# A longer opening in a new order, six column-halved weight blocks and paddings on two engines, in an attention-plus-bilinear-feed-forward kernel

## The chip, the cores and the metric

One core of a Trainium2 chip; the rounds of runs were on different chips, so a run is best compared with the kernel before in the same rounds (the ratio), and medians of different rounds only roughly. The metric is the device time of one execution in microseconds (us), of which a median is given. The granted clock is the share of full speed at which TensorE was let run; its mean over an execution is given where it matters. Engines: PE is TensorE (PEld its weight loads), DVE is VectorE, ACT is ScalarE, POOL is GpSimd, which issues the loads here, and SP is SyncE, which issues the DMA transposes. "Pair" means two attention heads of one batch: 4 pairs for each batch, 32 in all.

## The reference, cut to what matters

```python
# q, k, v: (batch 8, heads 8, seq 576, dim 64); bias_table: (32 buckets, 8 heads)
scores = matmul(q, k^T) / 8 + bias[head, bucket(|i - j|)]
attn   = softmax(scores);  attn_out = matmul(attn, v)
x   = attn_out as (4608 tokens, 512)
out = ((x @ w_a) * (x @ w_b)) @ w_out       # w_a, w_b: 512x1536, w_out: 1536x512
```

The softmax is computed as exp(score) times exp(bias); the exponentiated biases are read as sliding windows (tiles `W`) of a small table that the kernel itself writes to DRAM (`bias_tab`).

## The kernel before

Work runs in two parts. The opening (batch 0 and most of batch 1) is a list of tokens, issued in that order into each engine's queue. After it a loop over pairs takes over, which mixes attention steps with fixed numbers of feed-forward "units". Each engine's compute instructions run in the order of its queue; one that waits holds those behind it.

```python
    XG = [wpool.tile([128, 5, 2, Dh], BF16, name=f"XG{i}") for i in range(2)]   # attention output
    ...
    opening = """
        <k0 <q0 <q123h0 <tk <k23 <k1 <W0 <v0 <vtb <Wtb <W1 <W3 <vta <W2 <tq <R1 <q123h1 <v1 <R0 <Wta
        <wa0 <wb0 TK0 PD0 CK0:A PD1 w1 TQ0 PU1 CQ00:D CQ01:D w4 S000 w2 PU0 TQ20 E000 ...
        ... MT5 HA5b S62 E63 FA6b G5b MT6
        AV50 HA6b M63 E62 S60 FB6b N50 E60 FA7b G6b AV51 M62 HA7b FB7b M60 FA8f G7b N51 FB8f HA8f G8f
    """
    # <x: a load.  <W0..3: upper parts of the bias windows of pairs 0..3, <R0..3: the lower parts
    # S scores (PE), E exponentials (ACT), M bias products (DVE), T/ET/MT the same for the 64 tail
    # rows, AV attention times v (PE), N normalisation into XG (DVE), X transposes of XG (PE),
    # FA/FB products with w_a, w_b (PE), HA copy (ACT), G product (DVE), FO/HO w_out,
    # TH transposes of batch 2's q and k (DMA), w<n>: n filler matmuls on zeros
    # :A / :D: on ScalarE / VectorE.  FA3a, FA3b: column halves of weight block 3; FA8f: whole
    ...
    def av_norm(p, jqs):                     # token N: pav -> XG[p % 2]
        xg = XG[p % 2]
        ...
    def t_x(p, jqs=range(5), eng=None):      # XG -> xn, the feed-forward's input
        if 4 <= p < NP - 1 and p != 7:       # two DMA transposes, issued by SP
            nc.sync.dma_start_transpose(out=xn_sb[hp][...], in_=XG[p % 2][:, 0:4, :, :]...)
            nc.sync.dma_start_transpose(out=xn_sb[hp][...], in_=XG[p % 2][0:ST, 4, :, :]...)
            return
        tr_x(p, jqs); copy_x(p, jqs, eng)    # on PE, then a copy
    ...
    for s in range(7, NP + 1):               # loop step s: scores of pair s, av and N of pair s-1
        ...
```

Pair p writes its output to `XG[p % 2]`, and may do so only when pair p - 2's transposes have read it. And all DMA transposes stand in one queue, SP's, with batch 2's three transposes (`TH`: KB, QB, ZB) ahead of pair 5's.

The softmax here doesn't subtract the row's maximum and nothing guards it: scores larger than these inputs give would overflow.

Of the kernel before, what the change touches and what calls it, by code (L numbers as in the profile page):

```python
# [13 lines left out]
def kernel(  # L14
# [80 lines left out]
    vm = [wpool.tile([128, H, NM, Dh + 1], BF16, name=f"vm{i}") for i in range(2)]  # L95
    vt = [wpool.tile([128, H // 2, 2, Dh + 1], BF16, name=f"vt{i}") for i in range(2)]

# [70 lines left out]
    def load_vt(b):  # L168
        for hh in range(2):
            nc.gpsimd.dma_start(  # L170
                out=vt[b % 2][64 * hh:64 * hh + 64, :, hh, 0:Dh],
                in_=v[b, hh:H:2, SM:S, :].transpose([1, 0, 2]))
# [31 lines left out]

# [34 lines left out]

    nc.sync.dma_start(out=tab.ap(), in_=tab_sb[0:H, :])  # L240
    pad_vt(0)
    pad_ones(0)

# [5 lines left out]
    def load_vt_part(b, hh):  # L249
        nc.gpsimd.dma_start(  # L250
            out=vt[b % 2][64 * hh:64 * hh + 64, :, hh, 0:Dh],
            in_=v[b, hh:H:2, SM:S, :].transpose([1, 0, 2]))
# [85 lines left out]
    def copy_k(p, eng):  # L338
        copy(eng, KT[p % 4][:, :, :], st[p]["tk"][:, 0:SM].rearrange("d (t c) -> d t c", t=NM))

    def t_q(p, eng=None):
        if p >= NP or not early(p // 4):
            return
        ps = tr_half()
        transposes(ps, qn, p)
        copy(eng, QT[p % 4][:, :, :].rearrange("d a c -> d (a c)").rearrange("d (p t) -> d p t", t=NM),
             ps[:, 0:SM].rearrange("d (t p) -> d p t", t=NM))

    def t_k(p, eng=None, pool=None):
        if p >= NP or not early(p // 4):  # L350
            return
        ps = pool.tile([128, 1024], BF16, tag="ffn", name=f"trk{p}") if pool else tr_half()
        transposes(ps, kn, p)
        copy(eng, KT[p % 4][:, :, :], ps[:, 0:SM].rearrange("d (t c) -> d t c", t=NM))

# [198 lines left out]
    def av_mm(p, jqs, pool=None, tag="av"):  # L554
        b, hp = divmod(p, 4)
        i = b % 2
        pav = (pool or ps_av).tile([128, 3, 2, Dh + 1], FP32, tag=tag, name=f"av{p}_{jqs[0]}")
        for slot, jq in enumerate(jqs):
            nc.tensor.matmul(out=pav[:, slot, :, :], lhsT=weights_tail(p, jq),  # L559
                             rhs=vt[i][:, hp, :, :], start=True, stop=True)  # L560
            if jq == 4:
                for t in range(NM):
                    nc.tensor.matmul(out=pav[:, slot, :, :], lhsT=weights_last(p, t),  # L563
                                     rhs=vm[i][:, 2 * hp:2 * hp + 2, t, :], start=False,
                                     stop=True, skip_group_check=True)
# [25 lines left out]
    def t_x(p, jqs=range(5), eng=None):  # L591
        b, hp = divmod(p, 4)
        c0 = SM * B + ST * b
        if 4 <= p < NP - 1 and p != 7:
            nc.sync.dma_start_transpose(
# [95 lines left out]
    for c in range(NCH):  # L691
        if c == 0:
            parts = [(range(0, 8), 0, 256), (range(0, 8), 256, 256), (range(8, NDF), 0, 512)]
        else:
            parts = [(range(NDF), 0, 512)]
# [22 lines left out]
    def v_next(s):  # L718
# [9 lines left out]
    opening = """  # L728
        <k0 <q0 <q123h0 <tk <k23 <k1 <W0 <v0 <vtb <Wtb <W1 <W3 <vta <W2 <tq <R1 <q123h1 <v1 <R0 <Wta
        <wa0 <wb0 TK0 PD0 CK0:A PD1 w1 TQ0 PU1 CQ00:D CQ01:D w4 S000 w2 PU0 TQ20 E000 PC1 TQ10 S001 CQ20:D  # L730
        CQ10:D TQ30 E001 PC0 TZ1 CQ30:D S011 CZ1:A PC2 <vt1b <uq <vt1a <R2 <wa1 <q4 <R3 <k4 <wb1 <vb1b
        <q5 <k5 <uk <vb1a <wb2 <q6 <q7 <k6 <k7 <wa2 <wo S010 PF0 TK3 PF1 E011 TK2 CK3:D CK2:D E010 w1
        S300 M001 TK1 E300 M000 KS CK1:D EK w1 S101 V0:D E101 w1 S100 E100 M101 w1 S200 AV00 M300 E200 S301
        N00 TZ0 E301 M100 X00 S201 CX00:D AV10 wa4 E201 M200 N10 CZ0:A M201 X10 TQ11 M301 CX10:A T0 CQ11:A
        V1:D TQ31 ET0 S111 M010 AV20 E111 PW MT0 T1 N20 AV30 CQ31:A ET1 M011 TQ21 LH S110 N30 X20 CQ21:A
        S310 CX20:A MT1 X30 E110 AV01 CX30:D M111 FA0a E310 M110 S210 FB0a N01 HA0a S211 E210 FA1a G0a
        AV11 HA1a M210 E211 X01 T2 N11 TZ0x CX01:A T3 ET2 FB1a M211 X11 FA2a G1a CX11:A S311 MT2 HA2a
        FB2a ET3 CZ0x:D AV21 G2a E311 M310 TQ4 FA3a N21 CQ4:A TK4 FB3a HA3a CK4:D X21 FA4a G3a CX21:A
        S41 M311 HA4a S43 E41 MT3 FB4a FA5a E43 G4a AV31 LV M41 HA5a S40 V3:D S42 N31 E40 FB5a TQ5 G5a
        E42 X31 FA6a CQ5:D FB6a HA6a CX31:D TK5 G6a TZ1x CK5:A FA7a M40 FB7a HA7a CZ1x:D S52 S53 G7a E52  # L740
        FA0b V2:D FB0b M42 HA0b T4 E53 G0b FA1b M52 FB1b HA1b S50 M53 ET4 FA2b G1b TQ6 M43 HA2b S51
        CQ6:A FB2b MT4 E51 TQ7 G2b AV40 CQ7:D E50 TK6 M51 TK7 CK6:A FA3b M50 FB3b HA3b CK7:D S61 G3b T5
        E61 N40 FA4b FB4b HA4b M61 T6 ET5 G4b AV41 FA5b ET6 N41 TH S63 FB5b MT5 HA5b S62 E63 FA6b G5b MT6
        AV50 HA6b M63 E62 S60 FB6b N50 E60 FA7b G6b AV51 M62 HA7b FB7b M60 FA8f G7b N51 FB8f HA8f G8f
    """
# [4 lines left out]
    def step(token):  # L750
# [67 lines left out]
        elif kind == "N":  # L818
            av_norm(p, jqs)
            if not first and i[1] == 1:  # L820
                t_x(p)
        elif kind == "X":
            tr_x(p, jqs)
        elif kind == "CX":
            copy_x(p, jqs, eng)
        elif kind == "PU":
            pad_z(1, p)
        elif kind == "PF":
            nc.vector.memset(tl[0][64 * p:64 * p + 64, :, :, Dh - Dh * p:128 - Dh * p], 0.0)
        elif kind == "PC":  # L830
            if p == 2:
                pad_ones(1)
            else:
                nc.vector.memset(vt[1][64 * p:64 * p + 64, :, 1 - p, :], 0.0)
        elif kind == "PW":
            nc.vector.tensor_copy(out=Wt_sb[:, :, 0:64], in_=Wt_sb[:, :, 64:128])
        elif kind == "PD":
            pad_x(p)
        elif kind == "LH":
            load_half(2, 0)  # L840
            load_half(2, 1)
        elif kind == "TH":
            t_half(2, 0)
        elif kind == "LV":
            load_vt(2)
        else:
            raise ValueError(token)
# [4 lines left out]

    quotas = {7: 9, 8: 9}
    load_slot = {bb: 9 if bb == 3 else 12 if bb == 4 else 4 * bb - 5 for bb in range(3, B)}
    for s in range(7, NP + 1):
        new = s < NP
        U = "unit"
        A = lambda *jq: (lambda: av(s - 1, jq))
        steps = []
        if new:  # L860
            steps += [lambda: (qk(s, 0), ex(s, 0))]
        if new:
            head = [U, lambda: ex(s, 1), A(0, 1, 2), U, lambda: mul(s, 0), lambda: t_q(s + 1), U,
                    lambda: mul(s, 1)]
            late = [A(3, 4), lambda: t_x(s - 1), U]
            if s == 8:
                late = [A(3, 4), U, lambda: t_x(7, (0, 1, 2)), U, lambda: t_x(7, (3, 4))]
            if shared(s):
                pair = [lambda: v_next(s), lambda: (qk(s, 2), ex(s, 2), ex_rows(s)), U,
                        lambda: ex(s, 3), U, lambda: mul(s, 2), lambda: mul_rows(s)]  # L870
            else:
                pair = [lambda: v_next(s), lambda: (qk(s, 2), ex(s, 2)), U, lambda: ex(s, 3),
                        lambda: t_k(s + 1, ACT), U, lambda: mul(s, 2)]
            tail = [lambda: (qk_tail(s), ex_tail(s)), U, U, lambda: mul_tail(s)]
# [61 lines left out]
```

## Time and profile before

| | before |
|---|---|
| time, median of 3 | 416.77 us (416.66 to 417.65) |
| profiled span (an execution of 416.01 us, not one of the three) | 414.2 us |
| TensorE busy | 403.8 us, 97% |
| fillers on zeros | 22 matmuls |
| changes of the array's shape (rows x columns in use) from one matmul to the next | 177 |

The busy table and the chain of the page of the kernel before: engines with busy time, share and number of instructions; then the shares of the chain of work that ended last.

```profile
PE 403.8 (97%) x3497; PEld 210.9 (51%) x3497; DVE 241.1 (58%) x568; ACT 251.3 (61%) x388; POOL 133.5 (32%) x191
PE 90%; DMA 3%; POOL 2%; ACT 2%; issue 1%; ACTq 0%; DVE 0%
```

TensorE bounds the kernel. "97% busy" does not mean that only 3% can be won: the busy time of a matmul includes the run-out of its pipeline. The useful measure is from one matmul's start to the next one's. Here is one line of the timeline of the kernel before (start, duration, engine, line, operation, count):

```profile
71.86 1.89 PE L670 MATMUL po<-wo,g 128*128 128x512 bf16 x8
```

Eight matmuls of 512 columns take 1.89 us, of which the last one's own duration is 0.38 us: (1.89 - 0.38) / 7 = 0.216 us from start to start. The rest of the 0.38 us, 0.16 us, is run-out, which overlaps the next matmul.

The same kernel by stretches: us from the start, then length, and for each engine busy time and number of instructions, the granted clock, the DMA share and GB/s.

```profile
0.00:30.00 30.00, 24.56 (x330) 14.25 (x331) 21.73 (x65) 21.67 (x32) 22.51 (x36) 1.00 1.14 163
30.00:70.00 40.00, 39.22 (x472) 26.36 (x469) 33.45 (x87) 32.30 (x54) 24.90 (x35) 1.00 1.48 177
70.00:75.00 5.00, 5.00 (x30) 2.17 (x28) 2.59 (x8) 1.98 (x4) 0.78 (x2) 1.00 1.82 178
75.00:80.00 5.00, 5.00 (x61) 3.18 (x59) 3.13 (x9) 2.35 (x3) 1.22 (x2) 1.00 1.11 199
```

TensorE has gaps before 30 us and almost none after. So what a new order of this kind can win lies in the opening, a few us at most.

### The profile page before, as it was taken

To read this page: it belongs to the slowest core of one execution; us is meant where nothing else is said; L and a number is where in the kernel's file an instruction comes from. 1 tells how busy PE (TensorE), PEld (TensorE's weight loads), DVE (VectorE), ACT (ScalarE), POOL (GpSimd) and SP (SyncE) were. 2 spreads that over 40 slices of the span, in tenths; PEclk is the share of its full clock that TensorE was granted. 3 is DMA by queue.
4 is the path that set the end of the run, shared out by engine and by line. 5 is a ranking of instruction groups with operands and counts; after the bars stand their busy time and mean duration, and the time that the engine had idled before them with its cause. 6 is when DMAs were issued, how large, how long until landed. Compare 5 with 4: busy or idle time off the path is not lost.

```text
span 414.2 us, 8826 instructions
## 1 busy us (share of the span) xinstructions
PE 403.8 (97%) x3497; PEld 210.9 (51%) x3497; DVE 241.1 (58%) x568; ACT 251.3 (61%) x388; POOL 133.5 (32%) x191
## 2 busy tenths in 40 slices
PE   8789999999999999999999999999999999999996
PEld 3467664545454455544555555554545555444443
DVE  5778887466764665477646774567646652421320
ACT  4988876486647676676667665866476742322321
POOL 7956546399209500870059003400000000000000
PEclk9999999999999999999999999999999999999999
DMA  9999999999949943996099707940421012002004
GB/s 116 171 210 191 205 157 144 164 142 138 123 96 163 121 82 71 150 128 112 15 162 157 112 16 140 124 92 17 101 82 16 17 40 78 0 2 102 1 2 101
DMA packets 135786, 42.05 MB, mean 102 GB/s; under 512 B 113688, under 2 KB 130968, under 8 KB 135744
## 3 DMA queue, kind: packets, MB, share of 16 engines
q0 software_dynamic: 81712, 20.27, 54.6%
q1 hardware_dynamic: 48592, 11.87, 18.1%
q10 hardware_dynamic: 5440, 9.34, 6.8%
q8 instruction: 27, 0.44, 0.5%
q14 instruction: 15, 0.12, 0.1%
HBM read 39.18 MB, written 9.45 MB: 117 GB/s over the span
## 4 chain that ended last, share of the span: by engine, by line
PE 90%; DMA 3%; POOL 2%; ACT 2%; issue 1%; ACTq 0%; DVE 0%
PE pb L633 23%; PE pa L633 23%; PE po L670 22%; PE av L569 7%; PE qk L406 7%; DMA wb<-in_moe_w_b_dram 3%; PE av L559 2%; PE av L563 2%; PE qkt L479 1%; POOL W L235 1%; DMA bias_tab<-wo 1%; PE trb L306 1%; PE trb L415 1%; PE warm L220 1%; ACT att L514 1%
## 5 line engine op out<-in xcount | busy, mean ns | idle before, releaser
L430 ACT ACTIVATE at<-qk 128x1024 bf16<-128x1024 f32 x112 | 113.5, 1030 | 26.4 <-PE qk L406 10.6
L643 DVE TENSOR_TENSOR g<-pb,ha 128x512 bf16<-128x512 f32 (+1 forms) x116 | 75.9, 654 | 74.7 <-PE pb L633 46.8
L633 PE MATMUL pb<-xn,wb 128*128 128x512 bf16 (+1 forms) x464 | 112.5, 365 | 0.8 <-DMA wb<-in_moe_w_b_dram 0.8
L633 PE MATMUL pa<-xn,wa 128*128 128x512 bf16 (+1 forms) x464 | 112.5, 365 | 0.0
L640 ACT ACTIVATE ha<-pa 128x512 f32<-128x512 f32 (+1 forms) x116 | 66.7, 575 | 65.0 <-PE pa L633 65.0
L670 PE MATMUL po<-wo,g 128*128 128x512 bf16 x420 | 99.0, 379 | 0.0
L435 DVE TENSOR_TENSOR at<-at,W 128x1024 bf16<-128x1024 bf16 x112 | 74.8, 684 | 18.2 <-ACT at L430 18.2
L633 PEld LDWEIGHTS <-wa 128*128 128x128 bf16 x464 | 42.0, 98 | 46.2 <-issue 6.0
L633 PEld LDWEIGHTS <-wb 128*128 128x128 bf16 x464 | 41.4, 97 | 43.0 <-issue 4.7
L670 PEld LDWEIGHTS <-g 128*128 128x128 bf16 x420 | 38.7, 98 | 44.0 <-issue 2.5
L675 ACT ACTIVATE ob<-po 128x512 f32<-128x512 f32 x35 | 21.1, 601 | 40.7 <-PE po L670 34.4
L569 PE MATMUL av<-vm,at 128*128 128x65 bf16 x896 | 41.2, 194 | 0.0
L170 POOL DMA_DIRECT2D vt<-in_v_dram x12 | 7.4, 621 | 104.1 <-PE av L563 103.2
L580 DVE RECIPROCAL rc<-av 128x6 f32<-128x6 f32 (+1 forms) x64 | 11.9, 186 | 49.5 <-PE av L569 43.8
L569 PEld LDWEIGHTS <-at 128*128 128x128 bf16 x896 | 37.2, 98 | 6.2
L132 POOL DMA_DIRECT2D qn<-in_q_dram x48 | 36.8, 832 | 9.9 <-PE pb L633 6.8
L141 POOL DMA_DIRECT2D kn<-in_k_dram x48 | 36.4, 820 | 2.0 <-PE pb L633 1.4
L559 PE MATMUL av<-vt,att 128*128 128x130 bf16 x152 | 33.3, 219 | 0.0
L406 PE MATMUL qk<-QB,KB 64*128 64x512 bf16 x192 | 29.2, 381 | 0.2 <-ACT att L506 0.2
L582 DVE TENSOR_TENSOR XG<-av,rc 128x384 bf16<-128x384 f32 (+1 forms) x64 | 27.1, 424 | 2.2
L506 ACT ACTIVATE att<-qkt 128x640 bf16<-128x640 f32 x24 | 16.9, 702 | 12.9 <-PE qkt L480 12.9
L559 PEld LDWEIGHTS <-att 128*128 128x128 bf16 x152 | 15.0, 98 | 6.4
(104 smaller groups left out, 325.2 us busy)
## 6 DMA issues: line engine op xcount, KB each, us to landing
out_dram<-ob ACTq DMA_DIRECT2D x32, 256.0 KB, 2.6
vn<-in_v_dram POOLq DMA_DIRECT2D x16, 256.0 KB, 5.6
kn<-in_k_dram POOLq DMA_DIRECT2D x48, 64.0 KB, 4.6
qn<-in_q_dram POOLq DMA_DIRECT2D x48, 64.0 KB, 4.3
wa<-in_moe_w_a_dram POOLq DMA_DIRECT2D x3, 512.0 KB, 9.3
wb<-in_moe_w_b_dram POOLq DMA_DIRECT2D x3, 512.0 KB, 10.4
wo<-in_moe_w_out_dram POOLq DMA_DIRECT2D x1, 1536.0 KB, 15.5
xn<-XG SPq DMA_TRANSPOSE x52, 4.1
```

The source lines that it names most:

```text
L132: nc.gpsimd.dma_start(out=by_tile(qn[b % 2])[:, h0 // 4, t, :, :], in_=q[b, h0:h1, 128 * t:128 * t + 128, :].transpose([1, 0, 2]))
L141: nc.gpsimd.dma_start(out=by_tile(kn[b % 2])[:, h0 // 4, t, :, :], in_=k[b, h0:h1, t:SM:NM, :].transpose([1, 0, 2]))
L406: nc.tensor.matmul(out=ps[:, hh, :], lhsT=kT[r, t, :], rhs=qT[r, :, :], start=True, stop=True)
L430: nc.scalar.activation(out=at[:, :, :], in_=ps[:, :, :], func=ACTF.Exp, scale=scale)
L435: nc.vector.tensor_tensor(out=at[:, :, :], in0=at[:, :, :], in1=w[:, :, S - 1 + t:S - 1 + t - SM:-1], op=MULT)
L559: nc.tensor.matmul(out=pav[:, slot, :, :], lhsT=weights_tail(p, jq), rhs=vt[i][:, hp, :, :], start=True, stop=True)
L569: nc.tensor.matmul(out=pav[:, slot, hh, :], lhsT=weights(p, t, hh, jq), rhs=vm[i][:, 2 * hp + hh, t, :], start=False, stop=True, skip_grou ...
L582: nc.vector.tensor_tensor(out=xg[:, jqs[0]:jqs[0] + m, :, :], in0=pav[:, 0:m, :, 0:Dh], in1=rc[:, 0:m, :].unsqueeze(3).to_broadcast([128, ...
L633: nc.tensor.matmul(out=ps[:, 0:n], lhsT=w[df // 4][:, mc, 128 * (df % 4):128 * (df % 4) + 128], rhs=xn_sb[mc][:, 512 * c + lo:512 * c + lo ...
L640: nc.scalar.activation(out=ha[:, 0:n], in_=ff["pa", df, lo][:, 0:n], func=ACTF.Copy)
L643: nc.vector.tensor_tensor(out=g_sb[df][:, lo:lo + n], in0=ff["pb", df, lo][:, 0:n], in1=ff["ha", df, lo][:, 0:n], op=MULT)
L670: nc.tensor.matmul(out=po[:, :], lhsT=g_sb[df][:, 128 * tt:128 * tt + 128], rhs=wo_sb[:, df, :], start=(df == 0), stop=(df == NDF - 1))
```

## The change

Its intent: order the whole opening, now to the end of batch 1, by a list scheduler, so that TensorE has work at all times with fewer fillers; column halves only for six weight blocks; paddings with zeros on whichever of ScalarE and VectorE is free.

```diff
@@ paddings: a copy of zeros on ScalarE, or a memset on VectorE, as the token says
+    def pad(eng, x, p0, p1):
+        if eng is nc.vector:
+            nc.vector.memset(x, 0.0)
+            return
+        ... z = zero_sb (as fp32 where x is fp32), shaped like x
+        nc.scalar.activation(out=x, in_=z, func=ACTF.Copy)
@@ the ones of both buffers are set first
+    pad_ones(0)
+    pad_ones(1)
@@ pair 7 now has its own tokens (X70, X71: on PE, as before)
-        if 4 <= p < NP - 1 and p != 7:
+        if 4 <= p < NP - 1:
@@ six blocks in halves
-            parts = [(range(0, 8), 0, 256), (range(0, 8), 256, 256), (range(8, NDF), 0, 512)]
+            parts = [(range(0, 6), 0, 256), (range(0, 6), 256, 256), (range(6, NDF), 0, 512)]
@@ the opening, a new list (cut)
-        <k0 <q0 <q123h0 <tk <k23 <k1 <W0 <v0 <vtb <Wtb <W1 <W3 <vta <W2 <tq <R1 <q123h1 <v1 <R0 <Wta
-        <wa0 <wb0 TK0 PD0 ...
+        <k0 <q0 <q123h0 <k1 <k23 <vtb <W0 <tk <W2 <W1 <v0 <vta <W3 <tq <v1 <Wtb <q123h1 <R0 <Wta <k4 <R1
+        <wa0 <wb0 <R2 <uq <q4 ... PU0:A PV1:A PC1:A PF0:D TK0 PV0:A CK0:A PX1:D PF1:D w2 ...
+        HA0a T3 MT2 E210 AV11 CK4:D CX01:A S211 N11 FB0a ET3 FA1a G0a E211 X11 ...
+        V3:D HA5b M70 ET5 S71 N40 FB5b FA6f E71 MT5 G5b TQ6 HA6f M71 AV41 CQ6:A S73 N41 TH S72 E73 FB6f
+        E72 T6 M73 AV50 G6f ET6 M72 S62 FA7f N50 E62 MT6 AV51 HA7f M62 S61 S60 N51 E61 FB7f E60 S63 M61
+        FA8f G7f E63 M60 T7 HA8f FB8f M63 ET7 AV60 G8f FA9f MT7 N60 FB9f HA9f AV70 G9f FA10f N70 FB10f
+        HA10f AV71 G10f FA11f N71 FB11f HA11f X71 AV61 G11f X70 FO00 N61 FO01 CX71:D CX70:D FO02 HO0
@@ the loop starts one pair later; from step 9 on nothing differs
-    for s in range(7, NP + 1):
+    for s in range(8, NP + 1):
@@ (also: the layout of the value tails vt, and helpers that are no longer used)
```

More of the change, by code (lines that the diff above doesn't have):

```diff
@@ L95 @@
     vm = [wpool.tile([128, H, NM, Dh + 1], BF16, name=f"vm{i}") for i in range(2)]
-    vt = [wpool.tile([128, H // 2, 2, Dh + 1], BF16, name=f"vt{i}") for i in range(2)]
+    vt = [wpool.tile([128, 2, H // 2, Dh + 1], BF16, name=f"vt{i}") for i in range(2)]
     QT = [wpool.tile([128, NM, 128], BF16, name=f"QT{i}") for i in range(4)]
@@ L170, in load_vt @@
             nc.gpsimd.dma_start(
-                out=vt[b % 2][64 * hh:64 * hh + 64, :, hh, 0:Dh],
+                out=vt[b % 2][64 * hh:64 * hh + 64, hh, :, 0:Dh],
                 in_=v[b, hh:H:2, SM:S, :].transpose([1, 0, 2]))
@@ L191, in pad_tl, with pad_vt, pad_blocks, pad_x @@
         nc.vector.memset(tl[i][64:128, :, :, 0:Dh], 0.0)
-    def pad_vt(i):
-        nc.vector.memset(vt[i][0:64, :, 1, :], 0.0)
-        nc.vector.memset(vt[i][64:128, :, 0, :], 0.0)
+    def pad(eng, x, p0, p1):
+        if eng is nc.vector:
+            nc.vector.memset(x, 0.0)
+            return
+        n = int(np.prod(x.shape[1:]))
+        z = (zero_sb.bitcast(FP32) if x.dtype == FP32 else zero_sb)[p0:p1, 0:n]
+        if len(x.shape) == 3:
+            z = z.rearrange("p (a b) -> p a b", b=x.shape[2])
+        elif len(x.shape) == 4:
+            z = z.rearrange("p (a b c) -> p a b c", b=x.shape[2], c=x.shape[3])
+        nc.scalar.activation(out=x, in_=z, func=ACTF.Copy)
+    def pad_vt(i, hh, eng):
+        pad(eng, vt[i][64 * hh:64 * hh + 64, 1 - hh, :, :], 64 * hh, 64 * hh + 64)
+    def pad_blocks(x, hh, eng):
+        o = (Dh - Dh * hh) // 2
+        pad(eng, x.bitcast(FP32)[64 * hh:64 * hh + 64, :, :, o:o + Dh // 2], 64 * hh, 64 * hh + 64)
     def pad_ones(i):
-        nc.vector.memset(vt[i][0:64, :, 0, Dh:Dh + 1], 1.0)
-        nc.vector.memset(vt[i][64:128, :, 1, Dh:Dh + 1], 1.0)
+        nc.vector.memset(vt[i][0:64, 0, :, Dh:Dh + 1], 1.0)
+        nc.vector.memset(vt[i][64:128, 1, :, Dh:Dh + 1], 1.0)
         nc.vector.memset(vm[i][:, :, :, Dh:Dh + 1], 1.0)
-    def pad_x(i):
-        nc.vector.memset(XG[i][64:128, 4, :, :], 0.0)
+    def pad_x(i, eng):
+        pad(eng, XG[i][64:128, 4, :, :], 64, 128)
     nc.sync.dma_start(out=bt_sb[0:NB, :], in_=bias_table)
@@ L240 @@
     nc.sync.dma_start(out=tab.ap(), in_=tab_sb[0:H, :])
-    pad_vt(0)
-    pad_ones(0)
     def load_wt(hh):
@@ L250, in load_vt_part @@
         nc.gpsimd.dma_start(
-            out=vt[b % 2][64 * hh:64 * hh + 64, :, hh, 0:Dh],
+            out=vt[b % 2][64 * hh:64 * hh + 64, hh, :, 0:Dh],
             in_=v[b, hh:H:2, SM:S, :].transpose([1, 0, 2]))
@@ L339, in copy_k @@
         copy(eng, KT[p % 4][:, :, :], st[p]["tk"][:, 0:SM].rearrange("d (t c) -> d t c", t=NM))
-    def t_q(p, eng=None):
-        if p >= NP or not early(p // 4):
-            return
-        ps = tr_half()
-        transposes(ps, qn, p)
-        copy(eng, QT[p % 4][:, :, :].rearrange("d a c -> d (a c)").rearrange("d (p t) -> d p t", t=NM),
-             ps[:, 0:SM].rearrange("d (t p) -> d p t", t=NM))
-    def t_k(p, eng=None, pool=None):
-        if p >= NP or not early(p // 4):
-            return
-        ps = pool.tile([128, 1024], BF16, tag="ffn", name=f"trk{p}") if pool else tr_half()
-        transposes(ps, kn, p)
-        copy(eng, KT[p % 4][:, :, :], ps[:, 0:SM].rearrange("d (t c) -> d t c", t=NM))
     tz = {}
@@ L559, in av_mm @@
             nc.tensor.matmul(out=pav[:, slot, :, :], lhsT=weights_tail(p, jq),
-                             rhs=vt[i][:, hp, :, :], start=True, stop=True)
+                             rhs=vt[i][:, :, hp, :], start=True, stop=True)
             if jq == 4:
@@ L728 @@
     opening = """
-        <k0 <q0 <q123h0 <tk <k23 <k1 <W0 <v0 <vtb <Wtb <W1 <W3 <vta <W2 <tq <R1 <q123h1 <v1 <R0 <Wta
-        <wa0 <wb0 TK0 PD0 CK0:A PD1 w1 TQ0 PU1 CQ00:D CQ01:D w4 S000 w2 PU0 TQ20 E000 PC1 TQ10 S001 CQ20:D
-        CQ10:D TQ30 E001 PC0 TZ1 CQ30:D S011 CZ1:A PC2 <vt1b <uq <vt1a <R2 <wa1 <q4 <R3 <k4 <wb1 <vb1b
-        <q5 <k5 <uk <vb1a <wb2 <q6 <q7 <k6 <k7 <wa2 <wo S010 PF0 TK3 PF1 E011 TK2 CK3:D CK2:D E010 w1
-        S300 M001 TK1 E300 M000 KS CK1:D EK w1 S101 V0:D E101 w1 S100 E100 M101 w1 S200 AV00 M300 E200 S301
@@ L734 @@
-        N00 TZ0 E301 M100 X00 S201 CX00:D AV10 wa4 E201 M200 N10 CZ0:A M201 X10 TQ11 M301 CX10:A T0 CQ11:A
-        V1:D TQ31 ET0 S111 M010 AV20 E111 PW MT0 T1 N20 AV30 CQ31:A ET1 M011 TQ21 LH S110 N30 X20 CQ21:A
-        S310 CX20:A MT1 X30 E110 AV01 CX30:D M111 FA0a E310 M110 S210 FB0a N01 HA0a S211 E210 FA1a G0a
-        AV11 HA1a M210 E211 X01 T2 N11 TZ0x CX01:A T3 ET2 FB1a M211 X11 FA2a G1a CX11:A S311 MT2 HA2a
-        FB2a ET3 CZ0x:D AV21 G2a E311 M310 TQ4 FA3a N21 CQ4:A TK4 FB3a HA3a CK4:D X21 FA4a G3a CX21:A
@@ L739 @@
-        S41 M311 HA4a S43 E41 MT3 FB4a FA5a E43 G4a AV31 LV M41 HA5a S40 V3:D S42 N31 E40 FB5a TQ5 G5a
-        E42 X31 FA6a CQ5:D FB6a HA6a CX31:D TK5 G6a TZ1x CK5:A FA7a M40 FB7a HA7a CZ1x:D S52 S53 G7a E52
-        FA0b V2:D FB0b M42 HA0b T4 E53 G0b FA1b M52 FB1b HA1b S50 M53 ET4 FA2b G1b TQ6 M43 HA2b S51
-        CQ6:A FB2b MT4 E51 TQ7 G2b AV40 CQ7:D E50 TK6 M51 TK7 CK6:A FA3b M50 FB3b HA3b CK7:D S61 G3b T5
-        E61 N40 FA4b FB4b HA4b M61 T6 ET5 G4b AV41 FA5b ET6 N41 TH S63 FB5b MT5 HA5b S62 E63 FA6b G5b MT6
@@ L744 @@
-        AV50 HA6b M63 E62 S60 FB6b N50 E60 FA7b G6b AV51 M62 HA7b FB7b M60 FA8f G7b N51 FB8f HA8f G8f
+        <k0 <q0 <q123h0 <k1 <k23 <vtb <W0 <tk <W2 <W1 <v0 <vta <W3 <tq <v1 <Wtb <q123h1 <R0 <Wta <k4 <R1
+        <wa0 <wb0 <R2 <uq <q4 <q7 <k5 <q5 <R3 <wa1 <wb1 <k6 <vb1a <uk <vt1b <k7 <vt1a <wa2 <wb2 <vb1b
+        <q6 <wo PU0:A PV1:A PC1:A PF0:D TK0 PV0:A CK0:A PX1:D PF1:D w2 TQ0 PX0:A PU1:D CQ00:D PC0:D w2
+        S001 CQ01:A S000 E001 TQ20 TQ10 TK1 CQ10:A CQ20:D S011 E000 CK1:D TQ30 CQ30:A S100 E011 TK3 TK2
@@ new lines @@
+        CK3:D E100 S101 M001 TZ1 CK2:D E101 S301 M000 CZ1:D E301 w1 S201 M100 E201 w2 KS M101 EK w1 S200
+        M201 V0:D E200 S010 AV00 M301 E010 AV10 M200 TZ0 N00 S300 CZ0:A N10 E300 X00 V1:D X10 T0 CX00:D
+        AV20 CX10:A M300 ET0 TQ21 N20 TQ11 AV30 M010 CQ11:A CQ21:A S110 M011 PW:A S111 TQ31 LH E110 N30
+        X20 MT0 CX20:A T1 CQ31:D E111 AV01 M110 ET1 X30 M111 TK4 T2 N01 CX30:A S210 ET2 FA0a MT1 X01
+        HA0a T3 MT2 E210 AV11 CK4:D CX01:A S211 N11 FB0a ET3 FA1a G0a E211 X11 TZ0x M210 FB1a S310
@@ new lines @@
+        CZ0x:D HA1a S311 CX11:A G1a FA2a M211 E310 TQ4 TK5 MT3 AV21 HA2a CK5:D CQ4:A M310 FB2a E311 TQ5
+        G2a S43 CQ5:A N21 S42 FA3a E42 TQ7 M311 X21 FB3a HA3a CX21:D AV31 LV E43 G3a M42 FA4a CQ7:A M43
+        S41 HA4a S40 N31 E41 FB4a FA5a G4a E40 TK6 M41 X31 FB5a HA5a CX31:D S52 S53 G5a E52 FA0b M40
+        FB0b V2:D HA0b S51 G0b E53 FA1b CK6:D FB1b M52 HA1b TK7 E51 TZ1x G1b FA2b CZ1x:D FB2b HA2b S50
+        CK7:D FA3b G2b E50 M53 T4 FB3b M51 HA3b S70 ET4 G3b FA4b M50 FB4b HA4b T5 MT4 E70 FA5b G4b AV40
@@ L819, in step @@
             av_norm(p, jqs)
-            if not first and i[1] == 1:
+            if 4 <= p < 7 and i[1] == 1:
                 t_x(p)
@@ L825, in step @@
             copy_x(p, jqs, eng)
+        elif kind == "PV":
+            pad_vt(0, p, eng)
+        elif kind == "PC":
+            pad_vt(1, p, eng)
         elif kind == "PU":
-            pad_z(1, p)
+            pad_blocks(ZB[1], p, eng)
         elif kind == "PF":
-            nc.vector.memset(tl[0][64 * p:64 * p + 64, :, :, Dh - Dh * p:128 - Dh * p], 0.0)
-        elif kind == "PC":
-            if p == 2:
-                pad_ones(1)
-            else:
-                nc.vector.memset(vt[1][64 * p:64 * p + 64, :, 1 - p, :], 0.0)
+            pad_blocks(tl[0], p, eng)
+        elif kind == "PX":
+            pad_x(p, eng)
         elif kind == "PW":
-            nc.vector.tensor_copy(out=Wt_sb[:, :, 0:64], in_=Wt_sb[:, :, 64:128])
-        elif kind == "PD":
-            pad_x(p)
+            copy(eng, Wt_sb[:, :, 0:64], Wt_sb[:, :, 64:128])
         elif kind == "LH":
@@ L851 @@
     pad_tl(1)
-    quotas = {7: 9, 8: 9}
     load_slot = {bb: 9 if bb == 3 else 12 if bb == 4 else 4 * bb - 5 for bb in range(3, B)}
-    for s in range(7, NP + 1):
+    for s in range(8, NP + 1):
         new = s < NP
         U = "unit"
-        A = lambda *jq: (lambda: av(s - 1, jq))
+        A = lambda *jq: (lambda: av(s - 1, jq) if s > 8 else None)
         steps = []
@@ L862 @@
         if new:
-            head = [U, lambda: ex(s, 1), A(0, 1, 2), U, lambda: mul(s, 0), lambda: t_q(s + 1), U,
+            head = [U, lambda: ex(s, 1), A(0, 1, 2), U, lambda: mul(s, 0), U,
                     lambda: mul(s, 1)]
@@ L866 @@
             if s == 8:
-                late = [A(3, 4), U, lambda: t_x(7, (0, 1, 2)), U, lambda: t_x(7, (3, 4))]
-            if shared(s):
-                pair = [lambda: v_next(s), lambda: (qk(s, 2), ex(s, 2), ex_rows(s)), U,
-                        lambda: ex(s, 3), U, lambda: mul(s, 2), lambda: mul_rows(s)]
-            else:
-                pair = [lambda: v_next(s), lambda: (qk(s, 2), ex(s, 2)), U, lambda: ex(s, 3),
-                        lambda: t_k(s + 1, ACT), U, lambda: mul(s, 2)]
+                late = [U]
+            pair = [lambda: v_next(s), lambda: (qk(s, 2), ex(s, 2), ex_rows(s)), U,
+                    lambda: ex(s, 3), U, lambda: mul(s, 2), lambda: mul_rows(s)]
             tail = [lambda: (qk_tail(s), ex_tail(s)), U, U, lambda: mul_tail(s)]
@@ L893 @@
                     load_half(bb, g)
-        quota = quotas.get(s, 9)
+        quota = 9
         seen, put = 0, 0
```

## The prediction

> **What bounds the kernel.** TensorE. In the page's busy table PE is busy 403.8 of 414.2 us (ACT 251.3, DVE 241.1); PE holds 90% of the chain that ended last, at a clock of 1.000. Busy time hides loss, so I took matmul start to matmul start from the timeline: 512 columns take 216 ns, 256 take 109, 130 take 56, 65 take 33. At such rates all useful matmuls stream in about 373.4 us, the 22 filler matmuls on zeros in 4.7; about 29 us are lost between matmuls, 10.7 us of it before 30 us and 16.3 before 70. There are 177 changes of the array's shape (64-row pairs, transposes, full); in the steady part each costs 0.095 us, so 17 us in all. The Trainium skill, "TensorEngine Tiling (Array Packing)", Key Properties, says that changing the tiling mode drains the engine; the trace agrees (a 64x512 pair takes 212 ns, 308 where a full matmul follows).
>
> The other losses are waits: 1.2 us for first exponentials, 0.8 us for the first w_b block (landed near 27.9), many of 0.2 to 0.5 (list of waits).
>
> **What the change does**, by the order of instructions.
> - Column halves of blocks 6 and 7 are joined: 32 matmuls of 256 become 16 of 512. 2 x 109 against 216 ns: nothing. Useful stream stays 373.3 us.
> - Fillers fall from 22 to 15 (1.5 us), shape changes from 177 to 166 (1.0 us).
> - Paddings: ScalarE takes five, four of them between its first exponential (ends 3.2) and the first key copy (5.4), where it idles. The skill's "ScalarE: Activation LUTs" gives 186 ns + 0.833 ns per column; the trace's 64x256 copies take 0.38 us, so 1.6 us, nearly free.  VectorE gains about 1 us between 4 and 10 us.
> - One value-tail load fills 0.65 of the issuing queue's 1.44 us wait for the bias table. But a load of batch 1 now precedes the first w_a/w_b blocks, which may land up to 1 us later.
> - Before the first w_b unit stand 12.68 us of useful PE stream, formerly 10.64.
> - Pair 7's attention ends in the opening, not in loop steps 7 and 8; from step 9 on both programs are alike.
>
> **On the critical path.** At the first w_b unit: 2.0 us more work done, at most 1 us later, so 1.0 to 1.8 us ahead. From 30 to 80 us only about 5 us are lost, mostly shape changes; I expect 0.5 to 1 us there. Steady loop and end: unchanged.
>
> **Predicted: 414.4 us, 412.0 to 416.6 (8 in 10).** Faster by over 2%: 3%; within 2%: 96%; slower: 1%.
>
> **What would show it right.** The first w_b unit starts at 28 to 29 us with 2 us more stream behind it; first big exponential near 7.0 us (7.41 before); PE's loss before 30 us falls by 1 to 2 us; pair 9's first matmul starts about 2.4 us earlier, and the time from there to the end is equal within 0.3 us.
>
> **What would make it wrong.** Batch 1's tensors are wanted earlier: if their loads land late, or the queue is held up by the w_a/w_b landings, TensorE waits between 25 and 45 us and the gain is gone. ScalarE pads above 0.4 us would delay the first key copy. The other way: if most of the 8 us of waiting before 70 us goes, the time is below 412.

## More of the kernel before

SP's queue before (the issue of each DMA transpose), and after it two lines of VectorE: the first write of pair 7 into its buffer.

```profile
58.34 1.26 SPq L378 DMA_TRANSPOSE KB<-kn  x1
61.33 1.23 SPq L378 DMA_TRANSPOSE QB<-qn  x1
63.23 2.30 SPq L370 DMA_TRANSPOSE ZB<-tl  x1
65.63 2.04 SPq L595 DMA_TRANSPOSE xn<-XG  x1
67.76 1.20 SPq L598 DMA_TRANSPOSE xn<-XG  x1
...
76.25 0.20 DVE L580 RECIPROCAL rc<-av 128x6 f32<-128x6 f32 x1 [2.33 <-PE av L569]
76.47 0.56 DVE L582 TENSOR_TENSOR XG<-av,rc 128x384 bf16<-128x384 f32 x1
```

The lines at 65.63 and 67.76 are pair 5's transposes. By the trace they landed at 73.35 and 73.96 us; pair 7's write at 76.47 came 3.1 us after the first, which is the one that reads what it overwrites, and 2.5 us after the second, and so waited for nothing but its matmuls (the 2.33 us in brackets are for PE). Nothing in the list of waits shows this margin.

## The result, and the profile after

The changed kernel took 423.81 us (median of 4, 423.25 to 424.77), the kernel before 417.08 in the same rounds: slower by 1.6%. Ratios are computed as the mean time of one kernel's fast runs over that of the other's of the same rounds, so not quite the ratio of the medians quoted: here 1.0163, interval 1.0139 to 1.0186. The time lies far outside the predicted range of 412.0 to 416.6.

The same page lines for the changed kernel:

```profile
PE 402.5 (95%) x3423; PEld 210.6 (50%) x3474; DVE 238.3 (56%) x561; ACT 252.9 (60%) x391; POOL 133.6 (32%) x191
PE 86%; DMA 5%; POOL 3%; ACT 2%; DVE 1%; issue 1%; ACTq 0%; DVEq 0%
```

(51 matmul records are missing from this trace: 3423 against 3474 weight loads. A missing record looks like a gap of 0.2 us; none of the gaps discussed here is of that kind.)

By stretches:

```profile
0.00:30.00 30.00, 23.41 (x337) 14.33 (x338) 18.87 (x56) 23.45 (x37) 21.51 (x34) 1.00 1.09 152
30.00:70.00 40.00, 38.34 (x447) 24.28 (x451) 33.61 (x89) 32.54 (x52) 25.42 (x35) 1.00 1.48 181
70.00:75.00 5.00, 0.17 (x1) 0.00 (x0) 0.12 (x1) 0.00 (x0) 1.23 (x2) 0.96 1.71 157
75.00:80.00 5.00, 4.29 (x22) 2.31 (x24) 1.86 (x6) 0.60 (x1) 0.00 (x0) 0.50 0.29 24
80.00:85.00 5.00, 5.00 (x38) 2.85 (x37) 2.64 (x10) 0.60 (x1) 3.28 (x5) 0.85 0.53 55
```

Between 70 and 75 us all three compute engines stand still, and from 74.6 us on TensorE runs at half clock (the trace's record of the granted clock: 0.5 from 74.62 to 81.45 us; four matmuls of 512 columns that start at 78.27 us take 1.91 us there, and 1.03 at full clock). The first matmul of pair 9 starts at 93.67 us against 85.00; from there to the end it takes 329.30 us against 329.21. So the whole loss of 8.7 us lies before pair 9. (The profiled execution, of 424.77 us, is the slowest of the four, and that of the kernel before took only 416.01; the medians differ by 6.7 us.) The two starts, before and after, from TensorE's timeline:

```profile
85.00 0.39 PE L406 MATMUL qk<-QB,KB 64*128 64x512 bf16 x2
93.67 0.61 PE L406 MATMUL qk<-QB,KB 64*128 64x512 bf16 x4
```

What they waited for, SP's queue first, then VectorE and TensorE, from the timeline of the changed kernel:

```profile
59.60 1.26 SPq L378 DMA_TRANSPOSE KB<-kn  x1
62.47 1.24 SPq L378 DMA_TRANSPOSE QB<-qn  x1
64.41 2.04 SPq L370 DMA_TRANSPOSE ZB<-tl  x1
66.55 1.75 SPq L595 DMA_TRANSPOSE xn<-XG  x1
68.39 1.64 SPq L598 DMA_TRANSPOSE xn<-XG  x1
...
68.48 0.20 DVE L580 RECIPROCAL rc<-av 128x6 f32<-128x6 f32 x1 [0.19 <-PE av L569]
74.88 0.56 DVE L582 TENSOR_TENSOR XG<-av,rc 128x384 bf16<-128x384 f32 x1 [6.21 <-DMA xn<-XG]
75.50 0.29 PE L559 MATMUL av<-vt,att 128*128 128x130 bf16 x1 [5.33 <-DVE XG L582]
```

Pair 5's transposes are issued about as late as before (66.55 and 68.39 us, landing at 74.79 and 75.47), but pair 7's reciprocal is ready at 68.48, not at 76.25. Its write into the same buffer then waits 6.2 us. TensorE's next matmul needs the bank of PSUM (the memory into which matmuls write) that this instruction empties, and waits 5.3 us.

Two lists of waits of the changed kernel between 20 and 85 us show a second, smaller thing (waiter, what it waited for: us in total, times, longest; VectorE's first, then TensorE's):

```profile
DVE XG L582 <- DMA xn<-XG: 6.2, 1, 6.2
DVE att L530 <- DMA W<-bias_tab: 3.1, 1, 3.1
...
PE av L559 <- DVE XG L582: 5.3, 1, 5.3
PE trb L609 <- DVE XG L582: 1.1, 1, 1.1
PE pa L633 <- DMA wa<-in_moe_w_a_dram: 0.9, 1, 0.9
```

VectorE stood 3.1 us, up to 30.48 us, before pair 2's tail product (`MT2`), for the lower part of pair 2's bias window (`R2`). That is loaded behind the first two weight blocks and landed at 30.39 us. Behind `MT2` in VectorE's queue stands pair 1's normalisation, for which TensorE then waited 1.1 us. Before the change the same product came at 32.49 us and that load had landed at 29.06: no wait.

At the very start, the issuing queue of the kernel before and of the changed one:

```profile
7.07 0.72 POOL L235 DMA_DIRECT2D W<-bias_tab  x1 [1.44 <-DMA bias_tab<-wo]
```

```profile
8.32 0.72 POOL L252 DMA_DIRECT2D W<-bias_tab  x1 [2.75 <-DMA bias_tab<-wo]
```

The prediction counted only a load of batch 1 ahead of the weight blocks, not this. The first bias window was issued 1.25 us later, and with it everything behind it in that queue: the first w_a load at 18.79 against 16.69 us, the first w_b load at 19.84 against 17.43. TensorE's first w_b matmuls, before and after:

```profile
27.94 0.61 PE L633 MATMUL pb<-xn,wb 128*128 128x256 bf16 x4 [0.83 <-DMA wb<-in_moe_w_b_dram]
29.99 0.61 PE L633 MATMUL pb<-xn,wb 128*128 128x256 bf16 x4 [0.21 <-DMA wb<-in_moe_w_b_dram]
```

### The profile page after: what moved, and what is told of

It is laid out like the page before. It is cut to its first block, busy times and chain, and to the rows that moved or that the text cites. A ratio compares the mean times of both kernels' runs of the same rounds, so it can differ in the third digit from the quotient of the medians.

```text
span 423.0 us, 8721 instructions
## 1 busy us (share of the span) xinstructions
PE 402.5 (95%) x3423; PEld 210.6 (50%) x3474; DVE 238.3 (56%) x561; ACT 252.9 (60%) x391; POOL 133.6 (32%) x191
## 4 chain that ended last, share of the span: by engine, by line
PE 86%; DMA 5%; POOL 3%; ACT 2%; DVE 1%; issue 1%; ACTq 0%; DVEq 0%
PE pb L633 22%; PE pa L633 22%; PE po L670 21%; PE qk L406 7%; PE av L569 7%; DMA W<-bias_tab 2%; PE av L559 2%; DMA xn<-XG 2%; PE av L563 2%; PE qkt L479 1%; POOL W L252 1%; DMA bias_tab<-wo 1%; ACT ath L452 1%; PE trb L415 1%; PE warm L237 1%
## 5 line engine op out<-in xcount | busy, mean ns | idle before, releaser
L633 PE MATMUL pa<-xn,wa 128*128 128x512 bf16 (+1 forms) x438 | 111.3, 370 | 1.9 <-DMA wa<-in_moe_w_a_dram 0.9
L670 PE MATMUL po<-wo,g 128*128 128x512 bf16 x403 | 95.5, 379 | 0.8
L582 DVE TENSOR_TENSOR XG<-av,rc 128x384 bf16<-128x384 f32 (+2 forms) x64 | 27.2, 424 | 8.6 <-DMA xn<-XG 6.2
```

The lines of the kernel that those rows point to most:

```text
L582: nc.vector.tensor_tensor(out=xg[:, jqs[0]:jqs[0] + m, :, :], in0=pav[:, 0:m, :, 0:Dh], in1=rc[:, 0:m, :].unsqueeze(3).to_broadcast([128, ...
L633: nc.tensor.matmul(out=ps[:, 0:n], lhsT=w[df // 4][:, mc, 128 * (df % 4):128 * (df % 4) + 128], rhs=xn_sb[mc][:, 512 * c + lo:512 * c + lo ...
L670: nc.tensor.matmul(out=po[:, :], lhsT=g_sb[df][:, 128 * tt:128 * tt + 128], rhs=wo_sb[:, df, :], start=(df == 0), stop=(df == NDF - 1))
```

## The experiments

Theory A: the loss is pair 7's write waiting for pair 5's transposes, plus the low clock that the standstill brings. Rivals: the stall is only where general lateness shows (B), or the low clock is a cost of its own with another cause. For what is left after A: the load order, the paddings, the halves, or the wait for the bias window.

### 1. A third output buffer for pair 7

```diff
-    XG = [... for i in range(2)]
+    XG = [... for i in range(3)]      # its padding set once, on VectorE
+    def slot_x(p): return 2 if p == 7 else p % 2     # used wherever XG[p % 2] was
```

> The changed kernel with a third attention-output buffer, used by pair 7 alone. Theory A (pair 7's normalisation overwrites the buffer that pair 5's two DMA transposes still read; they land at 74.8 and 75.5 us, the write wants to start at 68.7; TensorE then stands 5.4 us and the granted clock falls to 0.5 for 6.8 us): the 6.2 us wait of VectorE on the transposes and the 5.3 us wait of TensorE are gone, the clock is 1.000, time 415 to 416.5 us. Rival B (the stall is only where lateness of the loads shows, and another wait takes its place, for instance on batch 2's transposes): the wait moves and the time stays above 419.

Measured: 416.22 us (415.69 to 416.73), ratio to before 0.9991 (0.9967 to 1.0016). The waits on the transposes are gone; in VectorE's timeline the reciprocal and the write now follow each other:

```profile
67.83 0.20 DVE L584 RECIPROCAL rc<-av 128x6 f32<-128x6 f32 x1 [0.19 <-PE av L570]
68.06 0.56 DVE L586 TENSOR_TENSOR XG<-av,rc 128x384 bf16<-128x384 f32 x1
```

The time is within the 415 to 416.5 that A gave, and B is out. One edit gives back 7.6 us by the medians (7.2 by the ratios 1.0163 and 0.9991). One part of the expectation failed: the clock of the profiled execution was 0.991, not 1.000. The half clock was now at the beginning, where pair 0's key tails landed late (a load that the change put behind the bias window). TensorE's line, and a stretch of this profile:

```profile
13.57 0.28 PE L362 MATMUL trb<-ident,tlc 64*128 64x64 bf16 x2 [2.64 <-DMA tlc<-in_k_dram]
```

```profile
13.60:17.00 3.40, 2.92 (x18) 1.41 (x20) 2.30 (x5) 2.05 (x2) 3.40 (x6) 0.50 1.38 166
```

This comes and goes: the four executions had clocks of 0.991, 1.000, 0.999 and 0.995, and 416.73, 415.80, 415.69 and 416.64 us.

### 2. The stall filled with matmuls on zeros

```diff
-        HA10f AV71 G10f
+        HA10f ws24 AV71 G10f          # 24 filler matmuls of 512 columns into a free PSUM bank
```

> The changed kernel with 24 filler matmuls of 512 columns (24 x 216 ns = 5.2 us) where TensorE stands still before pair 7's second half. The stall itself stays, but TensorE is kept active. Theory A with a separate clock cost: the clock stays 1.000 and the time falls by the half-clock cost alone, about 3 us, to 420.5 to 421.5. If the low clock costs nothing (or has another cause than the stall): 423.5 to 424.5.

Measured: 422.26 us (421.39 to 422.57), ratio to before 1.0139 (1.0113 to 1.0166). In the profiled execution the stall is still there for VectorE, but not the low clock. VectorE's wait and the two stretches:

```profile
DVE XG L582 <- DMA xn<-XG: 6.0, 1, 6.0
```

```profile
70.00:75.00 5.00, 4.95 (x25) 2.15 (x24) 0.70 (x2) 0.00 (x0) 1.25 (x2) 1.00 1.77 165
75.00:80.00 5.00, 4.95 (x50) 3.08 (x51) 3.60 (x14) 0.60 (x1) 1.44 (x3) 1.00 0.13 12
```

So the low clock at this place is a consequence of TensorE's standstill, and it costs time of its own. Between the two profiles, from the first w_b matmul (29.99 and 29.21 us) to pair 9 (93.67 and 90.28) the kernel with the filled stall is quicker by 2.6 us. The medians differ by only 1.6 us, less than the 2.3 to 3.3 expected, and by the ratios (1.0163 and 1.0139) by 1.0 us, with intervals that overlap; so the size rests on the two profiles. The execution with clock 1.000 took 421.39, the other three had low clocks of 0.992 to 0.996 again, and 421.99 to 422.57; where theirs fell is not recorded.

The Trainium skill, "TensorE: Matmul & The Clock Gate", What's actually happening, says that a monitor with a window of 3413 ns halves the clock after an idle window. The trace agrees: in the changed kernel the clock fell at 74.62 us, 4.5 us after TensorE's last matmul ended (70.17), and it stayed low for 6.83 us, in other profiles for 3.41.

### 3. Batch 2's transposes behind pair 5's

```diff
-        ... N41 TH S72 ...  ... N51 E61 ...
+        ... N41 S72 ...     ... N51 TH E61 ...
```

> The changed kernel with batch 2's first three DMA transposes moved behind pair 5's in the one transpose queue. Theory C (head of the line: pair 5's data is ready at 61.7 us, but its transposes wait in the queue until 66.55 us behind batch 2's, which wait for batch 2's loads): they are issued near 62 us, land near 67 to 68, and the stall shrinks to under 1 us, clock 1.000; batch 2's transposes come 2.5 us later, at 76 to 77 us, so a wait of 0 to 2 us may appear before pair 8's scores; time 415.5 to 418. Rival D (the transposes are slow only because the transfer engines are full): landing stays near 74 to 75 us and the time stays at 423 to 424.

Measured: 416.29 us (415.82 to 416.99), ratio 0.9995 (0.9971 to 1.0018). SP's queue with this order:

```profile
59.87 1.21 SPq L595 DMA_TRANSPOSE xn<-XG  x1
61.20 1.15 SPq L598 DMA_TRANSPOSE xn<-XG  x1
62.59 1.26 SPq L378 DMA_TRANSPOSE KB<-kn  x1
```

Pair 5's transposes, issued at 59.87 and 61.20 us, landed at 63.72 and 67.08; the stall is gone, and a wait of TensorE of 0.7 us for pair 8's first exponentials appears instead. Head of the line in one transpose queue (C) is right; D, that they are slow wherever they stand, is out as the main cause, but not as a part: the first lands 11.1 us earlier than in the changed kernel, of which 6.7 us are the earlier issue (some 1.5 of them because this execution was ahead by as much at the first w_b matmul) and 4.4 us a shorter transfer (3.9 against 8.2 us), and the second still took 5.9 us from issue to landing beside the loads of batch 2. The skill's "DMA: Bandwidth & Descriptors", Issuing engines are not separate DMA queues, says that transfers issued by different engines run on the same 16 DMA engines and interleave; that fits, but no run here takes the loads away.

### 4. The first loads in their former order

```diff
-        <k0 <q0 <q123h0 <k1 <k23 <vtb <W0 <tk <W2
+        <k0 <q0 <q123h0 <tk <k1 <k23 <W0 <vtb <W2
```

> The changed kernel with the order of the first loads as before: the small key-tail load ahead of the two key loads, the value-tail load behind the first bias window. Theory (the bias table's write waits behind bulk key loads: the queue's wait for it ends at 8.32 us instead of 7.07): the first bias window is issued near 7.1 us, the first w_a load near 17.3 instead of 18.8, the first w_b unit starts near 29 instead of 30 us, and the time falls by 0.5 to 1.5 us, to 422.3 to 423.3, while the stall stays. Rival (chance of the transfer engines, or something else holds the table's write): 423.3 to 424.3, queue's wait still ending after 8 us.

Measured: 422.94 us (421.69 to 424.91), ratio 1.0157 (1.0121 to 1.0193). The first bias window was issued at 7.80 us in the profile: earlier than 8.32, not 7.07 to 7.1. With a spread of 3 us the time tells nothing against 423.81. In all profiles of kernels with the changed kernel's first loads that issue lies at 7.53 to 8.32 us (four profiles), with this repair at 7.29 to 7.95 (seven), in the kernel before's order at 7.07 to 7.62 (three). A small effect is likely, its cost in time is not shown. The profile helps elsewhere: TensorE stood 4.9 us at pair 7, but the half clock lasted only 3.41 us. From the first w_b matmul (28.94 us) to pair 9 (90.66) it took 61.7 us against 63.7 in the changed kernel; 0.4 us of this is the shorter standstill, the other 1.6 us are about what 3.41 us less at half clock are worth (1.7 us by an estimate, half of 3.41).

### 5. Both repairs: third buffer and first loads

```diff
+    XG = [... for i in range(3)]; slot_x(p)                          # as in run 1
+        <k0 <q0 <q123h0 <tk <k1 <k23 <W0 <vtb <W2                    # as in run 4
```

> The changed kernel with both repairs: the third attention-output buffer for pair 7 and the first loads in their former order (key tails before the key loads). Theory: the buffer removes the 5.4 us stall and its low clock, and with the key tails loaded early no execution has the stall of 2.6 us at 10.9 to 13.6 us that the profile of the run with the buffer alone showed (key tails landed at 13.5 us, then half clock for 6.8 us). No wait of TensorE on the key-tail load, clock 0.998 or more in most executions, time 414.8 to 415.8, that is 0.1 to 0.4% below the kernel before. Rival (the reordered opening gains nothing by itself, its extra waits eat the shape changes saved): 416 to 416.8, equal to before.

Measured: 416.17 us (414.60 to 417.24), ratio 0.9978 (0.9952 to 1.0005). Not the 414.8 to 415.8 expected but in the rival's range, and inconclusive: the profiled execution (414.83 us) had clock 1.000 and no stall at the key tails, but two with clock 1.000 took 416.92 and 417.24. What makes them differ is not shown.

### 6. All paddings on VectorE

```diff
-        PU0:A PV1:A PC1:A ... PV0:A ... PX0:A        (on top of both repairs)
+        PU0:D PV1:D PC1:D ... PV0:D ... PX0:D
```

> As the run with both repairs, but all paddings on VectorE instead of five on ScalarE. If the move to ScalarE was nearly free and nearly worthless, as both engines wait at 3 to 7 us: within 0.3 us of the run with both repairs. If VectorE is what the first query copies wait for: 0.5 to 1 us longer, with the first exponential later than 7.1 us.

Measured: 416.02 us (415.82 to 416.76), ratio 0.9983 (0.9961 to 1.0005), against 0.9978 with the paddings on ScalarE. The placement of the paddings is worth nothing that these runs can see, as the prediction had it. In the changed kernel three pads of 260 columns took 0.40 to 0.42 us each on ScalarE, 0.33 and 0.41 us from start to start. An estimate from the figures of the Trainium skill, "ScalarE: Activation LUTs", What ACT_TABLE_LOAD costs, gives 403 ns for one alone, which agrees, and some 93 ns less from start to start back to back, which only the first of the two distances comes near.

### 7. Eight blocks in halves again

```diff
-        FA6f ... HA6f ... FB6f ... G6f               (on top of both repairs; block 7 likewise)
+        FA6a HA6a FB6a G6a FA6b ... HA6b ... FB6b ... G6b
```

> As the run with both repairs, but weight blocks 6 and 7 of the first chunk in two column halves again, done one after the other. If halves cost TensorE nothing (2 x 109 ns against 216): within 0.5 us, at most slightly longer from four more short evacuations on ScalarE and four on VectorE. If the halves matter: over 1 us longer.

Measured: 418.99 us (418.41 to 421.23), ratio 1.0063 (1.0036 to 1.0090): 2.8 us over run 5. The expectation was wrong. In the profile TensorE stands between these half units (at 56.43 and 57.62 us), for PSUM banks that ScalarE and VectorE have yet to empty:

```profile
PE pb L637 <- ACT ha L644: 0.5, 1, 0.5
PE pa L637 <- DVE g L647: 0.6, 1, 0.6
```

That is 1.1 us; what the rest of the 2.8 us is, the record does not show. The profiled execution is the slowest of the six (421.23 us) and also had the half clock for 6.83 us from 31.61 us on. Since the halves were put in one after the other without a new list, the run tells what a bad order costs, not what halves cost.

### 8. Control: the third buffer in the kernel before

```diff
+    XG = [... for i in range(3)]; slot_x(p)                          # as in run 1, on the kernel before
```

> Control: the kernel before with the third attention-output buffer for pair 7. There pair 5's transposes landed at 73.4 and 74.0 us and pair 7's first write began at 76.5 us, so the buffer was free 2.5 us before it was wanted: the time stays within 0.3 us of before (ratio 0.999 to 1.001). If the two-buffer scheme cost the kernel before anything, it gets faster by over 0.5 us.

Measured: 417.69 us (417.42 to 417.88), ratio 1.0019 (0.9995 to 1.0043). It does not get faster: before the change the two buffers cost nothing. It is a little slower than expected, within the interval; why is not followed up.

### 9. Transposes moved and first loads, no third buffer

```diff
+        ... N41 S72 ...     ... N51 TH E61 ...                       # as in run 3
+        <k0 <q0 <q123h0 <tk <k1 <k23 <W0 <vtb <W2                    # as in run 4
```

> The changed kernel with two repairs that only reorder: batch 2's transposes behind pair 5's, and the first loads in their former order; no third buffer. The run with the transposes moved gave 416.29 us with a wait of 0.7 us for pair 8's first exponentials; the former load order saved 0.3 to 0.9 us elsewhere. Expected 415.5 to 416.3. If the load order is worth nothing: 416.3 or more.

Measured: 417.19 us (415.34 to 417.86), ratio 1.0003 (0.9981 to 1.0025). A miss: not better than run 3. Four of its six executions had clocks of 0.990 to 0.998, and its profile (417.82 us) has a wait of TensorE of 1.2 us, up to 31.02 us, that the next run explains, and from 31.58 us on a half clock of 3.41 us.

### 10. Run 5 once more

The same program; no edit.

> The same program as the run with both repairs (third buffer, former load order), on another occasion, to tighten its ratio to before (0.9978, interval 0.9952 to 1.0005, executions from 414.6 to 417.2 us) and to see another execution's profile. If the reordered opening is worth 1 us: ratio 0.996 to 0.999 again. If the first was luck: 0.999 to 1.001.

Measured: 416.04 us (415.07 to 418.35), ratio 0.9993 (0.9966 to 1.0019). With run 5 it says: repaired in this way the reordered opening is worth 0.3 to 0.9 us by the two ratios, neither clear of zero, and not the 2.4 predicted. (In the two profiles pair 9 starts at 83.58 and 84.19 us, 1.4 and 0.8 us before the 85.00 of the kernel before.) Its profile shows where the rest is. VectorE, then TensorE:

```profile
29.31 0.43 DVE L531 TENSOR_TENSOR att<-att,W 128x512 bf16<-128x512 bf16 x1 [2.35 <-DMA W<-bias_tab]
31.02 0.59 PE L613 MATMUL trb<-ident,XG 128*128 128x128 bf16 x3 [1.32 <-DVE XG L586]
```

The wait for the bias window again (3.1 us in the changed kernel), and TensorE's wait behind it.

### 11. The kernel before with six halved blocks

```diff
-        ... FA6a CQ5:D FB6a HA6a ... G6a ... FA6b ...      (block 7 likewise)
+        ... CQ5:D ...                        ... FA6f ...
```

> The kernel before with only one part of the change: weight blocks 6 and 7 of the first chunk whole instead of in column halves, each at the place of its second half. TensorE's stream is the same (2 x 109 ns against 216 ns, 16 times); eight short evacuations become four longer ones; but 16 half-width matmuls (1.75 us) that filled TensorE from 42 to 46 us move to 57 to 60 us, where VectorE and ScalarE have other work. If that filling was not needed: 416 to 417, within 0.5 us of before. If it was: waits of TensorE of 1 to 2 us appear between 40 and 48 us and the time is 417 to 418.5.

Measured: 419.24 us (418.00 to 420.24), ratio 1.0053 (1.0033 to 1.0074). This part of the change alone makes the old list slower by 2.2 us (mean ratio times 416.65), more than the 417 to 418.5 us expected; TensorE stands, at 42.76 and 44.08 us, where the halves used to fill it:

```profile
PE trb L306 <- DVE xn L298: 1.1, 1, 1.1
PE qk L406 <- ACT KT L296: 0.7, 1, 0.7
```

So in this list the halves are worth something as early work, not as cheaper matmuls; a list made for six halves may do without the other two, as run 12 suggests.

### 12. Pair 2's tail product moved behind what TensorE needs

```diff
-        HA0a T3 MT2 E210 AV11 CK4:D CX01:A S211 N11 FB0a ET3 FA1a G0a E211 X11       (on run 5)
+        HA0a T3 E210 AV11 CK4:D CX01:A S211 N11 FB0a ET3 FA1a G0a MT2 E211 X11
```

> The run with both repairs, and pair 2's tail product on VectorE moved behind pair 1's normalisation and the first feed-forward product. In the changed kernel VectorE stood 3.1 us (2.35 us in the second profile of the repaired one) in that product, waiting for pair 2's bias window, which is loaded behind the first two weight blocks, and TensorE then waited 1.1 to 1.5 us for pair 1's normalisation behind it. Theory: those waits go (TensorE's wait for the normalisation near 30 us under 0.3 us, VectorE's wait for the window under 1 us), and the time falls by 0.5 to 1.3 us, to 414.8 to 415.6, ratio to before 0.996 to 0.998. If another wait takes its place (the first w_b block lands near 28 to 30 us anyway): 415.8 to 416.2, no gain.

Measured: 414.62 us (413.67 to 415.92), ratio 0.9952 (0.9933 to 0.9972): faster than the kernel before and than the changed one, and by the medians 1.4 to 1.6 us below runs 5 and 10 (the kernel before took 416.75 in these rounds, 416.59 and 416.65 in those); by the ratios 1.1 to 1.7 us, with intervals that overlap a little. VectorE around the first feed-forward product, and TensorE's transposes of pair 1:

```profile
27.92 0.20 DVE L584 RECIPROCAL rc<-av 128x6 f32<-128x6 f32 x1 [0.93 <-PE av L564]
29.02 0.42 DVE L647 TENSOR_TENSOR g<-pb,ha 128x256 bf16<-128x256 f32 x1
29.36 0.42 DVE L531 TENSOR_TENSOR att<-att,W 128x512 bf16<-128x512 bf16 x1
...
29.19 0.33 PE L613 MATMUL trb<-ident,XG 128*128 128x128 bf16 x3
```

No line has a wait for the window in brackets any more: it landed at 28.74 us, and the product, now last, starts at 29.36. TensorE's transposes run at 29.19 us without a wait. The first matmul of pair 9 starts at 82.73 us, 2.3 us before the 85.00 of the kernel before; from there to the end it takes 329.17 us. Part of the gain is probably the clock: all six executions had 0.999 or 1.000, while four of the twelve of runs 5 and 10 had 0.994 to 0.996, and in the profiles of runs 7 and 9 the half clock began at 31.61 and 31.58 us, in or just after the wait of TensorE that this edit removes. The profiled execution (413.67 us) is the fastest of the six.

## Why the prediction was wrong, and where it was right

**The step that failed** is the one on pair 7: "Pair 7's attention ends in the opening, not in loop steps 7 and 8; from step 9 on both programs are alike." The second half is right (329.21 and 329.30 us from pair 9 to the end). The first half was counted as a mere move. It brought pair 7's write from 76.5 to 68.7 us, while the release of its buffer, by DMA transposes at the end of a queue, did not come earlier with it: the first landed at 74.79 us, against 73.35 before. A margin of 3.1 us became a wait of 6.2. Run 1 (buffer) and run 3 (queue order) each remove the wait from its own side and take back 7.6 and 7.5 us by the medians. Run 2 shows that part of this is the clock.

The sum in the profiles, at pair 9, is 93.67 - 85.00 = 8.7 us: 5.3 us standstill of TensorE, about 2.6 us half clock (run 2), and some 0.8 us left over.

**The second step that failed** is the sum at the first w_b unit: "2.0 us more work done, at most 1 us later, so 1.0 to 1.8 us ahead." The unit began at 29.99 us, 2.05 us later than before, when its w_b block had landed (29.95 us against 27.89). That load was issued 2.41 us later: 1.25 us came with the first bias window, most of the rest with pair 4's keys, put ahead of w_a. So nothing was left of the lead in this execution. In the four profiles with these first loads the unit began at 28.46 (run 3) to 30.57 us (run 1), in the three with the kernel before's at 27.94 to 29.00; "at most 1 us later" held in some and not in others. The check on the first big exponential failed too: 7.64 us, for 7.0 predicted and 7.41 before. And a bias window wanted 3.1 us before it landed held VectorE's queue and then TensorE. Moving one token (run 12) recovers 1.4 to 1.6 us by the medians.

**What the prediction named as a risk** was of the right kind at the wrong place: late loads of batch 1, with waits from 25 to 45 us. There the waits were 1.1 us for the window and 0.9 us for w_a. The large one was at 70 us, for a buffer.

**What was right.** The gain in the list itself, though only in a kernel with three repairs: predicted 2.4 us at pair 9, and 2.3 us in run 12's profile. There the first w_b unit starts at 28.30 us, 0.4 us later than before with the 2.0 us more of work done that the prediction counted, so about 1.7 us ahead, within its 1.0 to 1.8. By the ratio the gain is 2.0 us. That run 12's 414.62 us lies next to the predicted 414.4 does not bear out the forecast for the kernel without repairs. "Within 2%" held for the changed kernel, but by other causes and with the other sign, which is luck. The paddings: nothing (runs 5 and 6). The steady loop: unchanged. That halving costs TensorE's stream nothing is not contradicted, but "nothing" was too much for the halves as a whole: taken alone they move the time by 2.2 us (run 11), through what fills TensorE.

**What stays open.** Why executions of one program differ by 2 to 3 us with clock 1.000 (run 5), how much of the time the load order is worth (run 4), how much of run 12's gain is the clock, and whether the third buffer and the load order are both needed beside the moved tail product, which was only run on top of them.

## What to carry to other kernels

When a schedule moves work earlier, list for every moved write what frees its buffer and for every moved read what fills it, with the time of landing from the trace; here the transfer kept its time when the compute moved, and the margin that there was before is in no list of waits. One blocked instruction at the head of an in-order queue also costs what stands behind it, so put what waits for a transfer last among equals. And a stall of TensorE of some us is to be counted with the half clock that may follow: here 5.3 us of standstill cost about 8 in the profile.

## What the Trainium skill lacked or had wrong

- "TensorE: Matmul & The Clock Gate", HAM oscillation: its rule is that no idle gap of TensorE should exceed about 3.4 us; that short idle times between groups of matmuls throttle too, the page also says, but with no figure for how thin is too thin. In the profile of run 1 the clock was halved from 11.74 us on, 0.8 us into a wait that lasted 2.64 us in all, and TensorE had been busy for 2.17 of the 3.41 us before; in runs 7 and 9 it was halved after 1.68 and 1.53 us of 3.41, with no wait above 1.2 us.
- The same page, Back-to-back issue gap: it gives about 131 ns for each 512-column matmul of a sustained stream and calls 216 ns the isolated gap. In this kernel's stream of weight loads and matmuls 512 columns took 216 ns, (1.89 - 0.38) / 7, which is what the page itself gives for back-to-back matmuls in another passage.
- "TensorEngine Tiling (Array Packing)", Key Properties: it says that a change of tiling mode drains the engine, but gives no cost. Here a change added about 0.095 us from matmul start to matmul start (84 changes after 105 us in the kernel before; where a matmul of 512 columns came before the change, 312 ns instead of 216).
- "DMA: Bandwidth & Descriptors": it has a bandwidth but no time for a small DMA transpose among bulk loads. Pair 5's, issued at 66.55 us beside batch 2's loads, took 8.2 us to land; issued at 59.87 us (run 3), 3.9 us.
